# ScalarE's copy of the scores of two steps on, put in front of the odd head's sign with the 32nd value

## The chip, the cores and the metric

One Trainium2 chip, one of its cores. The metric is device time in microseconds (us) of one execution. TensorE (PE) multiplies matrices into PSUM and transposes, VectorE (DVE), ScalarE (ACT) and GpSimd (POOL) work on elements, SyncE (SP) issues transfers. Each engine takes its instructions strictly in the order in which they were written for it; semaphores make one engine wait for another.

## The reference

Attention of 8 batches x 8 heads over 576 positions, head size 64, in which each query keeps only its 32 largest scores; then a mixture of 8 experts, one expert a token. Cut to what matters:

```python
scores = scale * np.matmul(q, k.transpose(0, 1, 3, 2))
kth = np.partition(scores, -32, axis=-1)[..., -32:-31]      # the 32nd largest of each row
scores = np.where(scores >= kth, scores, -1e9)
attn = np.exp(scores - scores.max(-1, keepdims=True))
attn = attn / (attn.sum(-1, keepdims=True) + 1e-9)
x = np.matmul(attn, v)                                      # then as (4608, 512) rows
...
e_idx = np.argmax(x @ w_gate, axis=1)                       # one expert of 8 a row
h = np.maximum(x[mask] @ w1[e], 0.0)
out[mask] = gate_w[mask, None] * eom[mask, e, None] * (h @ w2[e])
```

## The kernel before

**Tiles and steps.** The queries are cut into 36 tiles of 128 rows, and the 8 heads of a tile into 4 pairs, an even and an odd head each. One pass of the main loop, a step i of 144, starts the work of pair i and finishes that of the pairs before it. When a group of tiles is through, its rows are sent to the experts, and slots of 128 rows of one expert are worked between the attention of later tiles. Steps 0 to 39 come before the first slots; in the code they are `calm` (`i < LONE`, and `LONE` is 40). The change touches these alone.

**What a pair passes through.** TensorE multiplies queries and keys into the PSUM tile `ps` (`scores`, L282); there is only one such tile. ScalarE copies it to SBUF as `s`, both heads in one instruction of 128 x 1152 (the function that `scores` returns, L290); four `s` tiles take turns. VectorE takes the 8 largest of each of 8 pieces of a row (`gmax`, L309, 16 instructions) and ranks these into the largest 24 (`rank`, L317 and L320). With the 24th value as a bias ScalarE marks the elements near or above it and counts them (`below`, the sign L344, one for each head), GpSimd adds the marks to the scores (L347, into `w`), VectorE takes the 8 largest of the result (`window`, L359) and picks the 32nd value by the count (`spot` L370, `pick` L376, `choose` L382). GpSimd scales the row's largest value to the offset of the exponent (`shift`, L333), ScalarE forms exponentials (`exps`, L354).

For the even head VectorE multiplies the exponentials with the mask and sums them (`weigh`, L397). In the calm steps the odd head goes another way, that of `lone`: `choose` writes its 32nd value negated (`less`, L385); `veil` has ScalarE take the sign of score minus that value (L404) and GpSimd add it to the scores (L407, into `w`); a step later `unveil` has ScalarE form the exponentials of the result with their sum (L413). TensorE transposes the exponentials (`flip`, L424, in three parts; ScalarE copies each out, L432) and multiplies them with the values (`attend`, L456; ScalarE copies the result out as `xT`, L458).

**One calm step i on ScalarE**, as the code writes it: the two signs L344 of pair i, the first part's copy L432, `unveil(i - 2)` (L413), `exps(i)` (L354), in every other step the copy of `xT`, the second part's copy L432, in some steps small copies for the gates (L479, L489); then what the change touches: `veil(i - 1)` (L404) and what the list `last` holds, the copy of the scores of pair i + 2 (L290) and the third part's copy (L432).

**On the other engines.** TensorE, in the same step, has the middle part's transpose, which needs `unveil(i - 2)`, directly in front of the products L282 of pair i + 2. VectorE ends its step with `pick`, `choose` and `weigh` of pair i - 1 and begins the next with `rank` of pair i + 1. GpSimd ends the step with the add L407 of pair i - 1, and begins the next with `shift`, in some steps a scaling of output rows (L498), and the pair of adds L347:

```order
L387 COPY near_78<-v32_1358 128x4
L407 TENSOR_TENSOR w_1602<-s_1243,marks2_81 128x576
L333 TENSOR_SCALAR v32_1575<-v32_1575 128x2
L498 TENSOR_TENSOR xu_1287<-xu_1287,r_1286 128x256
L347 TENSOR_TENSOR w_1622<-s_1451,marks0_79 128x576
```

These rows of GpSimd, from the end of one step into the next (a second L347 follows), stand so in both kernels: whatever lets L407 start later holds up what is behind it.

The list `last` is filled and emptied in these lines:

```python
            if calm and i + 2 < NSTEP:
                last.append(scores(i + 2))
...
            if 1 <= i <= NSTEP:
                veil(i - 1)
            for f in last:
                f()
```

Of the kernel before, what the change touches and what calls it, by code (L numbers as in the profile page):

```python
# [38 lines left out]
def tile_topk_attention_moe(  # L39
# [152 lines left out]
    def run(exact, stack):  # L192
# [30 lines left out]
        def run_slow(budget, kinds):  # L223

            for x in [x for x in slow if x[2] in kinds]:
                if spent[0] + x[3] > budget:
                    return
                slow.remove(x)
                spent[0] += x[3]
                x[4]()  # L230
# [10 lines left out]
        def fill(n=1):  # L241
            for _ in range(n):
                if urgent:
                    urgent.popleft()()
                elif small and small[0]() is not False:
                    small.popleft()
# [24 lines left out]
        def scores(i):  # L271
            t, hp = divmod(i, NHP)
            ps = ps_s.tile([P, 2, 2, 512], F32, name="ps")
            two = len(TT[t]) == 2
            for n in range(2):
                cols = slice(n * 288, (n + 1) * 288)

                for m, (b, _) in enumerate(TT[t]):
                    qs = slice(m * 64, (m + 1) * 64) if two else slice(0, P)
                    for a in range(2):  # L280
                        rows = slice(a * 64, (a + 1) * 64)
                        nc.tensor.matmul(ps[qs, a, n, :288], Q[t][rows, hp, qs], K[b][rows, hp, cols],  # L282
                                         start=True, stop=True)
            s = wk.tile([P, 2, S], F32, name="s", bufs=4)
            for a in range(2):
                SC[i, a] = s[:, a, :]

            def copies(heads=((0, 2),)):
                for a0, a1 in heads:
                    nc.scalar.activation(s[:, a0:a1].rearrange("p a (n c) -> p (a n) c", n=2),  # L290
                                         ps[:, a0:a1].rearrange("p a n c -> p (a n) c")[:, :, :288], AF.Copy)
            return copies
# [18 lines left out]
        def rank(i, r):  # L311
            if exact:
                return
            vs, cs = VV[i]
            cs = [c.rearrange("p (g k) -> p g k", k=8)[:, :, :REACH[r]] for c in cs]
            for a in range(2):
                nc.vector.max(out=vs[:, a, 8 * r:8 * r + 8], in_=cs[a])  # L317
            if r < 2:
                for a in range(2):
                    nc.vector.match_replace(out=cs[a], in_to_replace=vs[:, a, 8 * r:8 * r + 8],  # L320
                                            in_values=cs[a], imm_value=LOW)
# [9 lines left out]
        def shift(i):  # L331
            vs = VV[i][0]
            nc.gpsimd.tensor_scalar(vs[:, :, 32], vs[:, :, 0], -SCALE, None, op0=ALU.mult)  # L333

        def below(i):
            vs = VV[i][0]
            ep = wk.tile([P, 2, S], F32, name="ep", bufs=3)
            EP[i] = ep
            if not exact:
                n = wk.tile([P, 2], F32, name="n", bufs=3)  # L340
                SW[i] = ([], n)
                for a in range(2):
                    s, m = SC[i, a], marks[a]
                    nc.scalar.activation(m.bitcast(I8).rearrange("p (s b) -> p s b", b=2)[:, :, 1], s, AF.Sign,  # L344
                                         bias=vs[:, a, PIVOT - 1:PIVOT], scale=-(1.0 + 2.0 ** -20), accum_out=n[:, a:a + 1])
                    w = wk.tile([P, S], F32, name="w", bufs=3)
                    nc.gpsimd.tensor_tensor(w, s, m, op=ALU.add)  # L347
                    SW[i][0].append(w)
# [474 lines left out]
        NSTEP = NTT * NHP  # L823
# [115 lines left out]
        for i in range(NSTEP + 4):  # L939
            t, hp = divmod(i, NHP)  # L940
            step[0] = i
            if i + 1 < NSTEP and (i + 1, 0) not in SC:
                scores(i + 1)()


            calm = i < LONE and not exact
            for r in range(3):
                if i < NSTEP:
                    rank(i, r)
                    if r == 0:  # L950
                        shift(i)
                if not calm:
                    fill(1)
            spent[0] = 0.0
            run_slow(SUMS, ("x",))
            spent[0] = 0.0
            if i < NSTEP:
                below(i)
            early, late, last = [], [], []
            mid, beside = None, None  # L960
            if calm and 2 <= i:
                first_copy = flip(i - 2, 0)
                mid = ps_t.tile([P, 4, P], F32, name="pst")
                f = side_start()
                beside = f(mid) if f else None
                first_copy()
            if 2 <= i < NSTEP + 2:
                unveil(i - 2)
            if calm:
                exps(i)  # L970
            if 4 <= i < NSTEP + 4 and i % 2 == 0:
                early.append(attend(i - 4))
            elif 2 <= i < LONE:

                idle = ps_m.tile([P, 4, P], F32, name="pm")
                for c in range(12 if beside else 24):
                    nc.tensor.transpose(idle[:, c % 4, :], ident, ident)
            if mid is not None:
                early.append(flip(i - 2, 1, beside, mid))
            elif 2 <= i < NSTEP + 2:  # L980
                early.append(flip(i - 2, 0))
                early.append(flip(i - 2, 1, side_start()))
            if calm and i + 2 < NSTEP:
                last.append(scores(i + 2))
            if i >= NSTEP + 2:
                extra = side_start()
                if extra:
                    early.append(extra(ps_t.tile([P, 4, P], F32, name="pst")))

            room = not uses  # L990
            ahead_of_slot()
            heavy_start()
            ev = heavy_piece()
            if ev:
                late.append(ev)
            if 2 <= i < NSTEP + 2:
                (last if calm else late).append(flip(i - 2, 2))
            ev = turn_ahead() if room or not heavy else None
            if ev:
                (last if calm else late).append(ev)  # L1000
            for f in early:
                f()
            if i < NSTEP and not calm:
                exps(i)
            for f in late:
                f()
            if 1 <= i <= NSTEP:
                spot(i - 1)
                window(i - 1, 0)
                window(i - 1, 1)  # L1010
            if i + 1 < NSTEP:
                gmax(i + 1, 0)
            if i + 1 < NSTEP:
                gmax(i + 1, 1)
            if 1 <= i <= NSTEP:
                pick(i - 1)
            if not calm:
                fill(1)
            if 1 <= i <= NSTEP:
                choose(i - 1)  # L1020
                fill(5 if calm else 1)
                weigh(i - 1)
            ahead("x", fetch_x, 2, "id", 1)
            run_slow(DMAS - 0.6 if calm else DMAS, ("ids", "out"))
            if 1 <= i <= NSTEP:
                veil(i - 1)
            for f in last:
                f()
            side_use()
            fill(3)  # L1030
            if i < NSTEP:
                if hp == 0 and t + 2 < NTT:
                    load_q(t + 2)
                if i == 0:
                    small.extend(([] if exact else setup()) + [clear_ids])
                jj = t % 9
                b2 = t // 9 * 2
                for j0, b in ((0, b2 + 1), (5, b2 + 2)):
                    n = (jj - j0) * NHP + hp
                    if b < NB:  # L1040
                        if n == 1:
                            load_k(b)
                        if n == 6:
                            load_v(b)
            if i >= 3 and (i - 3) % NHP == NHP - 1:
                tt = (i - 3) // NHP
                if tt == GROUPS[gi][0]:
                    LGT[gi] = st.tile([P, max(map(len, GROUPS)), 16], F32, name="lg", bufs=2)
                tile_rows(tt, gi, LGT[gi], tt - GROUPS[gi][0])
                if tt == GROUPS[gi][-1]:  # L1050
                    gi += 1
# [263 lines left out]
```

## Time and profile before

| | |
|---|---|
| time, median of 3 runs | 1270.94 us (1270.91 to 1271.02) |
| the profiled execution's own time | 1270.56 us |
| its span, first to last instruction | 1268.8 us |
| TensorE busy | 1178.6 us, 93% |
| VectorE busy | 1178.5 us, 93% |
| ScalarE busy | 1021.7 us, 81% |
| GpSimd busy | 692.0 us, 55% |
| the sign L404 | 40 instructions, 19.5 to 282.7 us |

A row of the timeline has the start and the duration in us, the engine, the line, the operation, out<-in and a count, and in brackets the idle time in front of it with what ended that. Where a row stands for several instructions, the duration is that of all of them. A row of the waits has who waited for whom, the total in us, how often, and the longest. A row of windows has a stretch in us, the busy time of each engine with the number of instructions, the granted TensorE clock and the share of the transfers. Instructions of one engine overlap at their ends by about 0.1 us, so the start of one to the start of the next is what it occupies.

### The profile page before, as it was taken

What the parts mean: (1) busy time and instruction counts of PE and PEld (TensorE: products, weight loads), DVE (VectorE), ACT (ScalarE), POOL (GpSimd) and SP (SyncE); (2) the same over time, 40 slices, a digit from 0 to 9 for tenths busy, and PEclk for the clock granted to TensorE, in tenths of its full rate; (3) what the DMA queues carried; (4) which work ended last, traced back from release to release, by engine and by line L of the source; (5) the groups of instructions that cost most, each with busy time, mean ns of one, the idle gap of its engine ahead of it and who ended that gap; (6) DMA issues with size and microseconds to landing.
All of it is one profiled execution on the core that took longest, in us unless ns stands there. A gap on an engine that the chain in (4) does not pass through costs nothing.

```text
span 1268.8 us, 30920 instructions
## 1 busy us (share of the span) xinstructions
PE 1178.6 (93%) x9769; PEld 894.7 (71%) x9769; DVE 1178.5 (93%) x6045; ACT 1021.7 (81%) x1958; POOL 692.0 (55%) x1048
## 2 busy tenths in 40 slices
PE   6887778879999999999999999999999999899996
PEld 5665555557777777777777777777777777678885
DVE  7999999999999999999999999999999994689984
ACT  6999999987888778878888888878888884388883
POOL 6666676674467665664564475456556663232110
PEclk8999999988999999999999999999999999899998
DMA  5400210237446555656557556554444445899981
GB/s 138 78 18 18 72 56 18 56 118 245 167 165 204 174 203 179 215 192 222 183 197 228 189 184 204 182 202 167 167 167 167 167 165 213 317 376 396 391 310 60
DMA packets 109376, 227.39 MB, mean 179 GB/s; under 512 B 14855, under 2 KB 33543, under 8 KB 108177
## 3 DMA queue, kind: packets, MB, share of 16 engines
q1 hardware_dynamic: 99824, 205.67, 47.0%
q0 software_dynamic: 7552, 18.96, 4.2%
q8 instruction: 79, 1.29, 0.4%
q10 hardware_dynamic: 1824, 0.67, 0.3%
q14 instruction: 97, 0.79, 0.2%
HBM read 206.68 MB, written 20.69 MB: 179 GB/s over the span
## 4 chain that ended last, share of the span: by engine, by line
DVE 66%; PE 15%; issue 11%; ACT 5%; POOL 1%; DMA 1%; DVEq 0%; POOLq 0%; SPq 0%; ACTq 0%
DVE cand L309 20%; DVE v L359 12%; DVE ep L397 11%; DVE cand L320 7%; DVE v L317 6%; PE pm L786 4%; PE po L456 3%; DVE x L376 2%; PE ps L282 2%; DVE x L370 2%; DVE kth L382 2%; PE pst L424 1%; PE pm L801 1%; PE pm L1107 1%; ACT marks L344 1%
## 5 line engine op out<-in xcount | busy, mean ns | idle before, releaser
L347 POOL TENSOR_TENSOR w<-s,marks 128x576 f32<-128x576 f32 x288 | 363.3, 1283 | 202.6 <-ACT marks L344 183.1
L309 DVE MAX8 cand<-s 128x8 f32<-128x72 f32 x2304 | 321.9, 216 | 12.9 <-ACT s L290 12.8
L424 PE MATMUL pst<-ident,ep 128*128 128x128 f32 x1296 | 206.3, 283 | 46.0 <-ACT ep L413 32.5
L344 ACT ACTIVATE marks<-s,v 128x576 int8<-128x576 f32 x288 | 220.6, 770 | 23.8 <-DVE v L317 21.7
L432 ACT ACTIVATE pT<-pst 128x512 f32<-128x512 f32 (+1 forms) x432 | 197.7, 483 | 51.8 <-PE pst L424 50.4
L424 PEld LDWEIGHTS pst<-ident,ep 128*128 128x128 f32 x1296 | 145.5, 141 | 132.9 <-issue 48.7
L786 PE MATMUL pm<-xs,w1t 128*128 128x128 f32 x1792 | 212.3, 277 | 0.0
L786 PEld LDWEIGHTS pm<-xs,w1t 128*128 128x128 f32 x1792 | 206.7, 194 | 0.2 <-issue 0.2
L359 DVE MAX8 v<-w 128x8 f32<-128x576 f32 x288 | 203.3, 746 | 0.0
L397 DVE SCALAR_TENSOR_TENSOR ep<-s,kth,ep 128x576 f32<-128x576 f32 x248 | 194.8, 817 | 8.6 <-DVE kth L382 0.5
L290 ACT ACTIVATE s<-ps 128x1152 f32<-128x1152 f32 (+1 forms) x145 | 162.2, 1120 | 50.3 <-PE ps L282 49.9
L801 PE MATMUL pm<-w2t,ht 128*128 128x512 f32 x432 | 194.4, 593 | 0.0
L456 PE MATMUL po<-pT,v 128*64 128x128 f32 (+3 forms) x3200 | 186.4, 268 | 0.0
L282 PE MATMUL ps<-kst,qst 64*128 64x288 f32 (+1 forms) x1280 | 179.5, 428 | 5.2 <-ACT s L290 5.2
L354 ACT ACTIVATE ep<-s,v 128x576 f32<-128x576 f32 x248 | 181.0, 779 | 3.1 <-POOL v L333 3.1
L456 PEld LDWEIGHTS po<-pT,v 128*64 128x64 f32 (+1 forms) x3200 | 159.0, 137 | 33.7 <-issue 31.9
L812 POOL DMA_INDIRECT out_dram<-y,idt x40 | 45.6, 1140 | 160.5 <-ACT y L808 147.8
L801 PEld LDWEIGHTS pm<-w2t,ht 128*128 128x128 f32 x432 | 78.0, 191 | 77.5 <-issue 77.5
L317 DVE MAX8 v<-cand 128x8 f32<-128x24 f32 (+2 forms) x864 | 132.2, 194 | 0.0
L282 PEld LDWEIGHTS ps<-kst,qst 64*128 64x128 f32 (+1 forms) x1280 | 97.0, 176 | 44.2 <-issue 17.5
L320 DVE MATCH_REPLACE8 cand<-v,cand 128x24 f32<-128x24 f32 (+1 forms) x576 | 97.5, 178 | 0.0
L333 POOL TENSOR_SCALAR v<-v 128x2 f32<-128x2 f32 x144 | 32.8, 227 | 113.8 <-DVE v L317 112.7
(185 smaller groups left out, 1689.6 us busy)
## 6 DMA issues: line engine op xcount, KB each, us to landing
w1t<-in_w_dram SPq DMA_DIRECT2D x40, 2048.0 KB
w2t<-in_w_dram SPq DMA_DIRECT2D x40, 2048.0 KB
v<-in_va_dram SPq DMA_DIRECT2D x8, 1152.0 KB
x_rows<-xu SPq DMA_DIRECT2D x36, 256.0 KB
qst<-in_qa_dram SPq DMA_DIRECT2D x70, 128.0 KB
kst<-in_ka_dram SPq DMA_DIRECT2D x14, 576.0 KB
ids<-far SPq DMA_DIRECT2D x1, 678.0 KB
xg<-x_rows,idt POOLq DMA_INDIRECT x40, 6.4
```

The costliest lines, as they stand in the source:

```text
L282: nc.tensor.matmul(ps[qs, a, n, :288], Q[t][rows, hp, qs], K[b][rows, hp, cols], start=True, stop=True)
L309: nc.vector.max(out=c[:, 8 * g:8 * g + 8], in_=SC[i, a][:, g * GW:(g + 1) * GW])
L317: nc.vector.max(out=vs[:, a, 8 * r:8 * r + 8], in_=cs[a])
L344: nc.scalar.activation(m.bitcast(I8).rearrange("p (s b) -> p s b", b=2)[:, :, 1], s, AF.Sign, bias=vs[:, a, PIVOT - 1:PIVOT], scale=-(1.0 ...
L347: nc.gpsimd.tensor_tensor(w, s, m, op=ALU.add)
L359: nc.vector.max(out=VV[i][0][:, a, 24:32], in_=SW[i][0][a])
L397: nc.vector.scalar_tensor_tensor(e, SC.pop((i, a)), kth_col(i, a), e, op0=ALU.is_ge, op1=ALU.mult, accum_out=SM[t][:, 2 * hp + a:2 * hp + ...
L424: nc.tensor.transpose(ps[:, c - c0, :], pt[:, c * P:(c + 1) * P], ident)
L432: nc.scalar.activation(x, ps[:, :n, :], AF.Copy)
L456: nc.tensor.matmul(po[a * 64:(a + 1) * 64, k, qs], lhs, rhs, start=half and not k and not m, stop=(c == 3 and k == 1 and m == len(TT[t]) - 1))
L786: nc.tensor.matmul(ph[:, f - f0, :], w[:, c, f * P:(f + 1) * P], XS[s][:, c, :], start=(c == 0), stop=(c == NC - 1))
L801: nc.tensor.matmul(PY[s], HT[s][:, f, :], w[:, f, :], start=(f == 0), stop=(f == NF - 1))
```

## The change

In the calm steps the first entry of `last`, which is the copy of the scores of pair i + 2, is called ahead of `veil(i - 1)`. The other entries stay behind it.

```diff
             ahead("x", fetch_x, 2, "id", 1)
             run_slow(DMAS - 0.6 if calm else DMAS, ("ids", "out"))
+            if last and calm and i + 2 < NSTEP:
+                last.pop(0)()
             if 1 <= i <= NSTEP:
                 veil(i - 1)
             for f in last:
                 f()
```

On ScalarE, at the end of the same step and into the next (the numbers are those of the tiles; `s_1243` is pair i - 1, `s_1563` pair i + 2), the kernel before has

```order
L354 ACTIVATE ep_1513<-s_1344,v32_1465 128x576
L432 ACTIVATE pT1_1557<-pst_1527 128x128
L404 ACTIVATE marks2_81<-s_1243,less_1596 128x576
L290 ACTIVATE s_1563<-ps_1558 128x1152
L432 ACTIVATE pT4_1569<-pst_1564 128x512
L344 ACTIVATE marks0_79,n_1620<-s_1451,v32_1575 128x576
```

and the changed one

```order
L354 ACTIVATE ep_1513<-s_1344,v32_1465 128x576
L432 ACTIVATE pT1_1557<-pst_1527 128x128
L290 ACTIVATE s_1563<-ps_1558 128x1152
L404 ACTIVATE marks2_81<-s_1243,less_1596 128x576
L432 ACTIVATE pT4_1569<-pst_1564 128x512
L344 ACTIVATE marks0_79,n_1620<-s_1451,v32_1575 128x576
```

The copy, which waits for TensorE's products, now stands ahead of the sign, which waits for VectorE's `less`; the sign has moved one place back. The same exchange is made 39 times, in steps 1 to 39; step 0 has no sign. The order on the other engines is the same in both kernels.

## The prediction

> **What bounds the kernel now.** I read the chain that ended last first, then busy time by stage, then the waits of each engine in the stage that the change touches (steps 0 to 39, up to about 276 us), and last one step instruction by instruction. The chain by engine, a stretch of the stage by windows (PE, PEld, DVE, ACT, POOL, then PE clock and DMA), and the waits there (total us, times, longest):
>
> ```profile
> DVE 66%; PE 15%; issue 11%; ACT 5%; POOL 1%; DMA 1%; DVEq 0%; POOLq 0%; SPq 0%; ACTq 0%
> ...
> 30.00:144.00 114.00, 91.75 (x944) 68.07 (x943) 112.49 (x684) 109.39 (x236) 76.81 (x102) 1.00 0.22 47
> ...
> DVE cand L309 <- ACT s L290: 0.6, 1, 0.6
> ...
> ACT marks L344 <- DVE v L317: 8.2, 11, 3.8
> ACT marks L404 <- DVE less L385: 6.4, 8, 1.8
> ...
> ACT s L290 <- PE ps L282: 0.7, 3, 0.2
> ```
>
> VectorE is busy 112.49 of 114 us and, from 30 to 340 us, waits once, 0.6 us. ScalarE is nearly as full, 109.39 of 114. So VectorE sets the pace and ScalarE has little room. The sign waits now and then for VectorE's negated 32nd value; the copy behind it hardly ever waits for its products (0.7 us in all), because the sign fills the time in which TensorE makes them.
>
> One step on ScalarE, with the starts of the same instruction one and four steps on:
>
> ```profile
> 47.95 0.78 ACT L344 ACTIVATE marks<-s,v 128x576 int8<-128x576 f32 x1
> ...
> 49.94 0.77 ACT L413 ACTIVATE ep<-w,v 128x576 f32<-128x576 f32 x1
> ...
> 50.70 0.77 ACT L354 ACTIVATE ep<-s,v 128x576 f32<-128x576 f32 x1
> ...
> 51.63 0.28 ACT L432 ACTIVATE pT<-pst 128x128 f32<-128x128 f32 x1
> 52.06 0.78 ACT L404 ACTIVATE marks<-s,less 128x576 int8<-128x576 f32 x1
> 52.74 1.11 ACT L290 ACTIVATE s<-ps 128x1152 f32<-128x1152 f32 x1
> 53.75 0.59 ACT L432 ACTIVATE pT<-pst 128x512 f32<-128x512 f32 x1
> 54.23 0.77 ACT L344 ACTIVATE marks<-s,v 128x576 int8<-128x576 f32 x1
> ...
> 67.36 0.78 ACT L344 ACTIVATE marks<-s,v 128x576 int8<-128x576 f32 x1 [0.31 <-DVE v L317]
> ...
> 73.99 0.78 ACT L344 ACTIVATE marks<-s,v 128x576 int8<-128x576 f32 x1
> ```
>
> Four steps take 73.99 - 47.95 = 26.04 us, 6.51 a step. The other engines in that step, and the two VectorE rows that go with 67.36:
>
> ```profile
> 50.86 0.33 PE L424 MATMUL pst<-ident,ep 128*128 128x128 f32 x1 [1.19 <-ACT ep L413]
> 51.12 1.24 PE L282 MATMUL ps<-kst,qst 64*128 64x288 f32 x8
> ...
> 52.98 1.28 POOL L407 TENSOR_TENSOR w<-s,marks 128x576 f32<-128x576 f32 x1 [1.44 <-ACT marks L404]
> 54.23 0.22 POOL L333 TENSOR_SCALAR v<-v 128x2 f32<-128x2 f32 x1
> 55.18 2.52 POOL L347 TENSOR_TENSOR w<-s,marks 128x576 f32<-128x576 f32 x2 [0.73 <-ACT marks L344]
> ...
> 67.14 0.61 POOL L498 TENSOR_TENSOR xu<-xu,r 128x256 f32<-128x256 f32 x1
> ...
> 52.62 0.26 DVE L317 MAX8 v<-cand 128x8 f32<-128x24 f32 x2
> ...
> 53.99 0.30 DVE L370 TENSOR_TENSOR x<-left,n 128x16 f32<-128x16 f32 x1
> 54.22 1.41 DVE L359 MAX8 v<-w 128x8 f32<-128x576 f32 x2
> 55.55 2.23 DVE L309 MAX8 cand<-s 128x8 f32<-128x72 f32 x16
> 57.70 0.16 DVE L376 TENSOR_TENSOR x<-x,v 128x16 f32<-128x16 f32 x1
> ...
> 65.95 0.26 DVE L317 MAX8 v<-cand 128x8 f32<-128x24 f32 x2
> ```
>
> The reader is to see two things. First, TensorE's products (L282) stand behind a transpose that starts only 0.92 us after the exponential L413 of the same step, so their end is tied to ScalarE itself. Second, VectorE's small compare L370 took 0.30 us and ended, at 54.29, with GpSimd's add L407 (52.98 + 1.28 = 54.26). That is no accident of one step:
>
> ```profile
> L370 DVE TENSOR_TENSOR x<-left,n x39: 157/303/868, 15.4 to 270.7; 128x16 f32<-128x16 f32 x39
> ...
> 30.00:276.00 246.00, 10.05 (x36) 0.98 0.17 42
> ...
> 277.20 1.29 POOL L407 TENSOR_TENSOR w<-s,marks 128x576 f32<-128x576 f32 x1
> ...
> 277.30 1.23 DVE L370 TENSOR_TENSOR x<-left,n 128x16 f32<-128x16 f32 x1
> ```
>
> (L370 alone: shortest, median and longest in ns, then its busy time in a window.) L370 needs 0.157 us and on average takes 10.05/36 = 0.28; where the add began 0.10 us ahead of it, it took 1.23 and ended at 278.53, the add at 278.49. A two-input VectorE instruction that meets a running GpSimd add waits for its end. The next instruction starts 0.04 ahead of that end (54.22 against 54.26).
>
> **The change, part by part.** No instruction is added or removed; 39 times the copy L290 and the sign L404 change places on ScalarE, and nothing moves on the other four engines or on the queues of transfers.
>
> The copy, first. From L344 (time 0) the exponential starts at 49.94 - 47.95 = 1.99; the transpose 0.92 later, the products 0.26 after it, and they last 1.24. A copy that waits for them starts 0.05 after their end:
>
> ```profile
> 262.00 1.24 PE L282 MATMUL ps<-kst,qst 64*128 64x288 f32 x8
> ...
> 263.29 1.14 ACT L290 ACTIVATE s<-ps 128x1152 f32<-128x1152 f32 x1 [0.24 <-PE ps L282]
> ```
>
> So it starts at 1.99 + 0.92 + 0.26 + 1.24 + 0.05 = 4.46. That is only 0.28 earlier than the 52.74 seen, for ScalarE comes free near 51.9 and now stands still until 52.41 with the sign queued behind. The earlier copy buys nothing: today's ends at 53.85 and its reader L309 starts at 55.55, 1.70 later.
>
> The sign, second. The copy occupies 1.01 (52.74 to 53.75), the sign starts at 5.47 and occupies 0.68 (52.06 to 52.74), the next copy 0.48 (53.75 to 54.23). The next L344 can start at 6.63 at the earliest, 0.12 above today's 6.51. In today's order the sign starts at 4.11; now it is 1.36 later, and GpSimd's add with it: it starts 0.92 after the sign (52.06 to 52.98), at 6.39, and ends at 7.67.
>
> The compare, third. L370 comes 1.37 after the step's first L317 (52.62 to 53.99), L344 1.41 after it where it waits for it (65.95 to 67.36), so L370 tries 0.04 ahead of L344. At steps of 6.63 that is 6.59, behind the add's start at 6.39: it is blocked to 7.67 instead of for today's tenth of a microsecond. This delays the next step's ranking, hence the next L344, which delays that step's sign. From the release to the following L344 VectorE needs one period less what lies between L317 and L359, plus 1.41. In the step shown that stretch is 54.22 - 52.62 = 1.60 with a compare of 0.30, so 1.58 on average: 6.51 - 1.58 + 1.41 = 6.34. An L344 therefore comes 7.67 - 0.04 + 6.34 = 13.97 after the one two steps earlier: 6.98 a step. This fits itself: 6.98 is above ScalarE's 6.63, and a compare at 6.94 still meets the add (6.39 to 7.67) and waits 0.73. The cost is 0.47 a step, 39 x 0.47 = 18.3 us.
>
> Against that stands the routing work, which lengthens some steps on VectorE alone:
>
> ```profile
> 14.02 0.30 DVE L317 MAX8 v<-cand 128x8 f32<-128x24 f32 x2
> ...
> 275.93 0.27 DVE L317 MAX8 v<-cand 128x8 f32<-128x24 f32 x2
> ```
>
> Steps 1 to 39 last 261.91 us, 8.0 more than 39 x 6.51. While L370 is blocked, such work fills the wait: in the two-step sum it counts half. One step holds some 3.8 of it (the longest wait for L317 above), which can save no more than about one block, 0.7; of the other 4.2 half is saved, 2.1. The sum is 18.3 - 2.8 = 15.5 us.
>
> Costed at nothing: the later L333 (to 7.86, so 0.88 after the next L344; its reader L354 starts 2.75 after it); the later w for L413, 1.3 us in hand; L376, which comes 3.48 after L359, at about 4.1 after L344, where the pair L347 ends at 0.95 + 2.52 = 3.5, or at 4.0 in steps where the scaling L498 (0.61) stands between L333 and it. That last cover is thin, about 0.1; where it is gone L376 is blocked by the rest of the pair.
>
> The bounds of the one unknown, the copy's start: if the products were ready when ScalarE is free (3.95), the add ends at 7.16, the step is 6.73, and with half of the routing work saved the total is +6; if they always ran at the low clock below, each start is 1.05 later. I take 4.46, whose rows are of this very stage.
>
> On GpSimd's durations the Trainium skill (Perfetto Trace Analysis, GPSIMD Engine Instruction) says that reported spans are unreliable and start-to-start spacing is to be used. By that the add takes 1.25 (52.98 to 54.23), and the sum is 0.6 lower; by the row at 277.30 the span holds to 0.04.
>
> The delay should reach the end whole: VectorE has 66% of the chain and the later steps hang on it. Against the profiled execution's 1270.56 us (the median of the runs is 0.38 above) this gives 1286.
>
> **The rivals.**
>
> *Only ScalarE's own loop counts.* If the add and the compare settle so that they don't meet, a step is 6.63: at most 39 x 0.12 = 4.7, and the 8.0 of routing work lets ScalarE catch up. That gives 1271 to 1275. For it: ScalarE's lag has 1.7 us of cover at L309. Against it: at 6.63 the compare falls 0.20 behind the add's start. Chance 10%, two thirds of it within 0.2%, which is about what a measurement can tell from no change.
>
> *Faster.* The compare passes ahead of the add, and its waits go: (0.28 - 0.157) x 39 = 4.8 us, 1266. It decides at a compare ahead of 6.39, a step of at most 6.43, which needs the products 0.2 earlier than their rows. Chance 5%.
>
> *TensorE's clock falls.* Longer steps leave it idle for longer. Its clock did fall once after a thin stretch, and products then took 2.29:
>
> ```profile
> 226.00:229.00 3.00, 1.99 (x19) 1.75 (x17) 3.00 (x17) 2.49 (x7) 1.84 (x4) 1.00 0.02 5
> 229.00:232.00 3.00, 2.09 (x13) 1.25 (x13) 2.86 (x19) 1.78 (x6) 1.63 (x4) 1.00 0.00 0
> ...
> 235.00:238.00 3.00, 3.00 (x32) 3.00 (x32) 2.93 (x21) 2.53 (x6) 2.59 (x3) 0.52 0.68 186
> ...
> 290.24 2.29 PE L282 MATMUL ps<-kst,qst 64*128 64x288 f32 x8
> ```
>
> That puts the add 1.05 later, 0.53 a step: in half of the steps 10 us more, 1296, in all 1307. Chance 10%. The Trainium skill (TensorE: Matmul & The Clock Gate, HAM oscillation) has the clock fall only after idle gaps beyond about 3.4 us; by that it would not fall here and this rival had no chance. The rows differ: the two slices before the fall were idle for 1.01 and 0.91, no gap of 3.4.
>
> *The swap does nothing* needs ScalarE to take the two out of order; no row shows that, and it goes with the first rival.
>
> **How the numbers follow.** The forecast has 75%, the three rivals 10, 5 and 10. Slower by over 0.2% is the forecast, the clock's rival and a third of the first: 0.75 + 0.10 + 0.03 = 0.88; same is the rest of the first, 0.07; faster 0.05. The range runs from the low bound of the copy's start, +6, to the forecast with the clock down in a third of the steps: 1277 to 1293.
>
> **What would show it.** In the changed profile, in this stage: L290 waits for L282 in most steps, about 0.5 us; L404 no longer waits for L385; L370's median is near 0.9 us, and its ends lie 0.03 behind those of L407; the stage's steps are near 7.0 us; L309 waits no more than now. If L370 stays near 0.3 the third step of the sum is wrong; if L290 doesn't wait, the first. A granted clock well below 0.98 speaks for the third rival.

## The result and the profile after

The changed kernel takes 1286.78 us (median of 4 runs, 1285.30 to 1288.65) against 1270.93 (1270.37 to 1271.02): 15.9 us or 1.26% slower, ratio 1.0126, 95% interval 1.0109 to 1.0144. The forecast was 1286.0. The profiled execution took 1287.09, its span is 1285.3, 16.5 longer than the span before. "Stage" below means the time from the first L317 of the first row here to that of the second, as in the prediction; it went from 261.91 to 278.40, by the same 16.5. The delay arises there and is carried to the end whole. The stage's ends on VectorE, in the timeline of the changed kernel:

```profile
13.96 0.30 DVE L317 MAX8 v<-cand 128x8 f32<-128x24 f32 x2
...
292.36 0.27 DVE L317 MAX8 v<-cand 128x8 f32<-128x24 f32 x2
```

The chain by engine on the page of the profile, and a stretch by windows (PE, PEld, DVE, ACT, POOL, then PE clock and DMA):

```profile
DVE 68%; PE 15%; issue 10%; ACT 4%; POOL 1%; DMA 1%; DVEq 0%; POOLq 0%; SPq 0%; ACTq 0%
```

```profile
30.00:144.00 114.00, 85.39 (x834) 62.71 (x834) 112.69 (x630) 102.51 (x220) 73.39 (x100) 1.00 0.22 46
```

VectorE is as busy as it was, 112.69 of 114 us, yet it issues 630 instructions there instead of 684. It does not wait more; its instructions have become longer. ScalarE was busy 109.39 and is now busy 102.51. Its waits in the changed kernel from 14 to 290 us (total, times, longest):

```profile
ACT s L290 <- PE ps L282: 19.3, 35, 1.0
ACT marks L344 <- DVE v L317: 12.6, 20, 4.1
...
ACT marks L404 <- DVE less L385: 0.8, 1, 0.8
```

The copy now waits for its products in 35 steps, 0.55 each, and the sign no longer waits for `less`. These are ScalarE's waits. Where VectorE's time went is read from its groups of the stage (count, total us, mean ns, idle before). Before:

```profile
L397 DVE SCALAR_TENSOR_TENSOR ep<-s,kth,ep 128x576 f32<-128x576 f32 x39 | 31.2, 801 | 0.0
...
L370 DVE TENSOR_TENSOR x<-left,n 128x16 f32<-128x16 f32 x39 | 11.7, 300 | 0.0
L376 DVE TENSOR_TENSOR x<-x,v 128x16 f32<-128x16 f32 x39 | 7.0, 179 | 0.0
```

After:

```profile
L397 DVE SCALAR_TENSOR_TENSOR ep<-s,kth,ep 128x576 f32<-128x576 f32 x39 | 33.7, 864 | 0.0
...
L370 DVE TENSOR_TENSOR x<-left,n 128x16 f32<-128x16 f32 x39 | 21.8, 560 | 0.0
L376 DVE TENSOR_TENSOR x<-x,v 128x16 f32<-128x16 f32 x39 | 13.2, 340 | 0.0
```

The compare L370 costs 10.1 us more, the pick L376 6.2, the weighting L397 2.5, and two small routing instructions (L581, L627) 2.2 less: 16.6 in all, against 16.5 of the stage. All other large groups on VectorE are as before within 0.1 us. So the whole growth of VectorE's time lies in instructions that read two operands from SBUF. Whether that is the cause of the loss, or only what VectorE does while ScalarE is late, these sums can't say; the experiments are to decide it.

One step of the changed kernel, across the engines:

```profile
100.47 0.76 ACT L413 ACTIVATE ep<-w,v 128x576 f32<-128x576 f32 x1
...
101.63 1.24 PE L282 MATMUL ps<-kst,qst 64*128 64x288 f32 x8
...
102.98 1.13 ACT L290 ACTIVATE s<-ps 128x1152 f32<-128x1152 f32 x1 [0.83 <-PE ps L282]
...
104.01 0.77 ACT L404 ACTIVATE marks<-s,less 128x576 int8<-128x576 f32 x1
...
104.92 1.28 POOL L407 TENSOR_TENSOR w<-s,marks 128x576 f32<-128x576 f32 x1 [2.23 <-ACT marks L404]
...
105.20 1.04 DVE L370 TENSOR_TENSOR x<-left,n 128x16 f32<-128x16 f32 x1
```

The products end at 102.87, the copy follows 0.11 later, the sign 1.03 after that, GpSimd's add another 0.91, and 0.28 into the add comes the compare. It ends at 106.24, the add at 106.20. This is the prediction's picture. But 14 of the 39 compares took 0.16 us, and in ten of these steps the pick is caught instead:

```profile
169.73 0.16 DVE L370 TENSOR_TENSOR x<-left,n 128x16 f32<-128x16 f32 x1
...
170.33 1.28 POOL L407 TENSOR_TENSOR w<-s,marks 128x576 f32<-128x576 f32 x1 [3.57 <-ACT marks L404]
170.56 0.78 ACT L344 ACTIVATE marks<-s,v 128x576 int8<-128x576 f32 x1
...
171.75 2.52 POOL L347 TENSOR_TENSOR w<-s,marks 128x576 f32<-128x576 f32 x2
...
173.29 1.01 DVE L376 TENSOR_TENSOR x<-x,v 128x16 f32<-128x16 f32 x1
```

ScalarE is so late here that the compare passes ahead of the add. But L344 is then late as well: it comes 0.83 after the compare instead of 0.04. GpSimd's pair of adds L347 runs until 174.27, and the pick runs into it and ends at 174.30. Six steps in a row, from 31 to 67 us, went this way, and four later ones; in three the weighting was caught. In those six steps L344 never waits; the next one follows after 6.69 us each time, and after the last of them after 6.90.

```profile
36.60 0.78 ACT L344 ACTIVATE marks<-s,v 128x576 int8<-128x576 f32 x1
...
43.29 0.78 ACT L344 ACTIVATE marks<-s,v 128x576 int8<-128x576 f32 x1
```

There ScalarE's own loop sets the pace, and VectorE's wait at the pick costs nothing.

### The profile page after: what moved, and what is told of

It is laid out like the page before. It is cut to its first block, busy times and chain, and to the rows that moved or that the text cites. A ratio compares the mean times of both kernels' runs of the same rounds, so it can differ in the third digit from the quotient of the medians.

```text
span 1285.3 us, 30922 instructions
## 1 busy us (share of the span) xinstructions
PE 1180.2 (92%) x9769; PEld 893.9 (70%) x9769; DVE 1194.8 (93%) x6045; ACT 1022.7 (80%) x1958; POOL 691.1 (54%) x1048
## 4 chain that ended last, share of the span: by engine, by line
DVE 68%; PE 15%; issue 10%; ACT 4%; POOL 1%; DMA 1%; DVEq 0%; POOLq 0%; SPq 0%; ACTq 0%
DVE cand L309 21%; DVE v L359 12%; DVE ep L397 11%; DVE cand L320 7%; DVE v L317 6%; PE pm L786 5%; DVE x L376 3%; PE po L456 3%; DVE x L370 3%; PE ps L282 2%; DVE kth L382 2%; PE pst L424 1%; PE pm L801 1%; PE pm L1109 1%; ACT marks L344 1%
## 5 line engine op out<-in xcount | busy, mean ns | idle before, releaser
L347 POOL TENSOR_TENSOR w<-s,marks 128x576 f32<-128x576 f32 x288 | 363.0, 1282 | 187.0 <-ACT marks L344 169.1
L309 DVE MAX8 cand<-s 128x8 f32<-128x72 f32 x2304 | 321.9, 216 | 13.6 <-ACT s L290 13.6
L344 ACT ACTIVATE marks<-s,v 128x576 int8<-128x576 f32 x288 | 220.6, 770 | 26.5 <-DVE v L317 24.7
L397 DVE SCALAR_TENSOR_TENSOR ep<-s,kth,ep 128x576 f32<-128x576 f32 x248 | 197.3, 827 | 8.6 <-DVE kth L382 0.5
L317 DVE MAX8 v<-cand 128x8 f32<-128x24 f32 (+2 forms) x864 | 132.1, 194 | 0.0
L407 POOL TENSOR_TENSOR w<-s,marks 128x576 f32<-128x576 f32 x40 | 51.3, 1281 | 81.1 <-ACT marks L404 81.0
```

The source lines that it names most:

```text
L309: nc.vector.max(out=c[:, 8 * g:8 * g + 8], in_=SC[i, a][:, g * GW:(g + 1) * GW])
L397: nc.vector.scalar_tensor_tensor(e, SC.pop((i, a)), kth_col(i, a), e, op0=ALU.is_ge, op1=ALU.mult, accum_out=SM[t][:, 2 * hp + a:2 * hp + ...
```

## The experiments

The theory put to the test: GpSimd's adds end later because the sign starts later, and an instruction of VectorE with two operands in SBUF waits for them. The rival: ScalarE's 19.3 us of waiting for products is the loss, and the blocked instructions only fill time that VectorE would spend waiting anyway. "Regular step" is the mean of steps 9 to 20: 6.54 us in the kernel before, 7.07 in the changed one. Times are medians of at least 4 runs, beside runs of the kernel before on the same chip (medians 1270.06, 1270.44 and 1270.78).

**The waits taken away: products ahead of the middle transpose.** In the changed kernel (e3_early_after) and, as a control, in the kernel before (e4_early_before):

```diff
+            if calm and i + 2 < NSTEP:
+                last.append(scores(i + 2))
             if mid is not None:
                 early.append(flip(i - 2, 1, beside, mid))
...
-            if calm and i + 2 < NSTEP:
-                last.append(scores(i + 2))
```

> The change, and TensorE makes the products of pair i + 2 ahead of the middle part's transpose, so that they don't hang on the exponential L413. Theory (the price is VectorE's compare and pick meeting GpSimd's later adds): ScalarE's waits for products, 19.3 us in the changed kernel, go; the copy starts near 3.9 us after L344, the add runs from 5.8 to 7.1, the compare at 6.66 still meets it, a step is (7.1 - 0.04 + 6.34)/2 = 6.70: about 1276 us, and L370 still takes clearly more than 0.157 us. Rival (the 19.3 us of waiting on ScalarE are the loss of 16 us): all of it comes back, 1271 us.

> The kernel before, with the same earlier products and the sign still ahead of the copy. The copy hardly waited for products there (0.7 us in all), and the add starts when it did. Both theories: 1270 to 1272 us. It shows what the earlier products do by themselves.

The first took 1284.69 us (two runs at 1280 and 1281, two at 1288; ratio 1.0125, 1.0095 to 1.0156), the second 1283.84 (1.0104, 1.0087 to 1.0121). A wait of ScalarE and a group of VectorE in the first, whose profiled execution was the fastest of its four:

```profile
ACT marks L344 <- DVE v L317: 16.9, 27, 3.3
```

```profile
L370 DVE TENSOR_TENSOR x<-left,n 128x16 f32<-128x16 f32 x39 | 20.8, 533 | 0.0
```

The copy's wait for products is gone from the list, and the time is not back. The regular step is 6.75, where the theory had 6.70. The compare still takes 20.8 us in all, and L344 waits for VectorE 27 times, where it waited 20 times in the changed kernel. The totals of both forecasts were missed, for the edit has a price of its own. In the control the copies of the transposed weights wait for a transpose that now stands behind the products, and every fourth regular step is longer, up to 9.07 us:

```profile
ACT pT L432 <- PE pst L424: 19.3, 21, 1.8
```

So the waits went and the loss stayed, but since the edit by itself costs the control 13.8 us, the pair of runs doesn't decide between theory and rival.

**The block taken away: the compare's operands in PSUM.** Steps 0 to 39 keep the constant and the result of the compare in PSUM. An idle tile was freed for it (the filling transposes write to another). The edit was made in the kernel before (e11_psum_before) and in the changed one (e12_psum_after):

```diff
+        held = ps_m.tile([P, 4, P], F32, name="pm")
+        nc.vector.tensor_copy(held[:, 0, :8], left)
...
-            X8[i] = wk.tile([P, 2, 8], F32, name="x8", bufs=2)
-            nc.vector.tensor_tensor(X8[i], left[:, None, :].to_broadcast([P, 2, 8]),
+            near_by = step[0] < LONE
+            if near_by:
+                X8[i] = held[:, 1 + i % 2, :16].rearrange("p (a k) -> p a k", a=2)
+            else:
+                X8[i] = wk.tile([P, 2, 8], F32, name="x8", bufs=2)
+            nc.vector.tensor_tensor(X8[i], (held[:, 0, :8] if near_by else left)[:, None, :].to_broadcast([P, 2, 8]),
```

> The kernel before, with the constant of the compare L370 and the result of compare and pick kept in a PSUM tile in the calm steps, so that compare and pick read only one operand from SBUF (the pm tile is free there once TensorE's filling transposes write into po). The same instructions in the same order. Theory: a VectorE instruction is blocked by GpSimd's adds only when it reads two operands from SBUF; the 0.12 us of blocking a step go: 1265 to 1271 us, L370 all alike. Rival: 1271 us.

> The change, with compare and pick reading one operand from PSUM in the same way. ScalarE's order and its waits for products stay (about 20 us). Theory (the loss is VectorE blocked by the later adds): what is left is ScalarE's loop of 6.63 us a step, caught up in the steps with routing work: 1271 to 1277 us. Rival (the 20 us of waits for products are the loss): 1286 us.

The kernel before gains 5.4 us by it (1265.08; ratio 0.9958, 0.9941 to 0.9974), the changed one 9.9 (1276.88; 1.0054, 1.0037 to 1.0071). The groups of the first, in which the weighting is L403:

```profile
L403 DVE SCALAR_TENSOR_TENSOR ep<-s,kth,ep 128x576 f32<-128x576 f32 x39 | 31.2, 801 | 0.0
...
L376 DVE TENSOR_TENSOR pm<-pm,n 128x16 f32<-128x16 f32 x39 | 6.4, 164 | 0.0
```

The groups and a wait of the second (compare L376, pick L382):

```profile
L403 DVE SCALAR_TENSOR_TENSOR ep<-s,kth,ep 128x576 f32<-128x576 f32 x39 | 41.5, 1065 | 0.0
...
L376 DVE TENSOR_TENSOR pm<-pm,n 128x16 f32<-128x16 f32 x39 | 6.4, 164 | 0.0
L382 DVE TENSOR_TENSOR pm<-pm,v 128x16 f32<-128x16 f32 x39 | 6.4, 163 | 0.0
```

```profile
ACT s L290 <- PE ps L282: 21.5, 36, 1.6
```

This refutes the rival for the larger part of the loss. ScalarE keeps the changed order and waits 21.5 us for products, and 9.9 of the 15.9 us are back; 1276.88 is the upper end of the theory's range.

What is left is ScalarE's own loop, as the theory had it, and in this loop the waits for products do count. The first L344 of each step, in three steps in a row, without an idle time in front:

```profile
82.49 0.78 ACT L344 ACTIVATE marks<-s,v 128x576 int8<-128x576 f32 x1
...
89.18 0.78 ACT L344 ACTIVATE marks<-s,v 128x576 int8<-128x576 f32 x1
...
96.08 0.78 ACT L344 ACTIVATE marks<-s,v 128x576 int8<-128x576 f32 x1
```

It comes every 6.69 us, and after 6.90 in every fourth step; the forecast for this loop was 6.63. From 30 to 250 us it does not wait for VectorE at all here. In the changed kernel it does, in the same stretch:

```profile
ACT marks L344 <- DVE v L317: 6.2, 15, 0.9
```

So the exchange lengthens two loops, and in the changed kernel the one through VectorE's blocked instructions is the longer. With compare and pick freed the kernel runs at ScalarE's pace. That is why the exchange still costs 11.8 us between these two kernels: the regular step is 6.37 us in the first and 6.75, at ScalarE's pace, in the second. The stages differ by 11.5 (254.86 and 266.40).

The block itself is not gone in the second. Compare and pick run free in both, but the next instruction with two operands in SBUF, the weighting, has grown by 10.3 us:

```profile
97.84 2.51 POOL L347 TENSOR_TENSOR w<-s,marks 128x576 f32<-128x576 f32 x2
...
98.98 0.16 DVE L382 TENSOR_TENSOR pm<-pm,v 128x16 f32<-128x16 f32 x1
...
99.45 1.52 DVE L403 SCALAR_TENSOR_TENSOR ep<-s,kth,ep 128x576 f32<-128x576 f32 x1
...
100.30 0.72 POOL L393 COPY near<-v 128x4 f32<-128x4 f32 x1
```

The pick runs in 0.16 us in the midst of the pair of adds; the weighting has to wait for the pair's end at 100.35 and ends 0.62 later. The block passes on to the next such instruction. But since L344 does not wait for VectorE in this stretch, this block sets no pace and is not the cause of the 11.8 us.

On this the Trainium skill (SBUF — State Buffer, Who interferes with whom) says that a VectorE instruction with two SBUF inputs and a GpSimd instruction that reads SBUF exclude each other, while one with at most one SBUF input, outside certain fast modes, doesn't contend. The runs agree: the compare took 560 ns on average in the changed kernel and 164 ns once one operand was in PSUM.

**The sign later still.** In the changed kernel the sign goes behind the third part's copy as well, about half a microsecond (e5_sign_last):

```diff
             if last and calm and i + 2 < NSTEP:
                 last.pop(0)()
+                if last:
+                    last.pop(0)()
```

> The change taken one place further: the third part's copy L432 also stands ahead of the sign. ScalarE has the same instructions and the same loop through the products; only the sign, and with it the add, comes 0.48 us later (add 6.87 to 8.15 us after L344). Theory: a step is (8.15 - 0.04 + 6.34)/2 = 7.22 us, 0.24 more than forecast for the change: about 1295 us. Rival: the waits for products are the same, so the time stays at that of the change, 1287 us.

It took 1290.80 us (1286.57 to 1294.30; ratio 1.016, 1.0131 to 1.0189). The regular step is 7.28, where the theory had 7.22, with ScalarE's wait for products unchanged (20.2 us). The median is 4.0 above the changed kernel's, half of what the theory gave, and the two ranges overlap. Its groups:

```profile
L376 DVE TENSOR_TENSOR x<-x,v 128x16 f32<-128x16 f32 x39 | 20.1, 516 | 0.0
L370 DVE TENSOR_TENSOR x<-left,n 128x16 f32<-128x16 f32 x39 | 18.2, 466 | 0.0
```

More compares pass ahead of the add (the one at 105.85 took 0.16, the add came at 105.98), and the pick pays. The longer regular step is that of one profiled execution; the times alone don't separate this kernel from the changed one.

**The adds in four pieces**, so that a block would last a quarter, in the changed kernel (e8_split_after) and, as a control, in the kernel before (e9_split_before):

```diff
-                    nc.gpsimd.tensor_tensor(w, s, m, op=ALU.add)
+                    for c in range(4 if i < LONE else 1):
+                        k = slice(c * 144, (c + 1) * 144) if i < LONE else slice(0, S)
+                        nc.gpsimd.tensor_tensor(w[:, k], s[:, k], m[:, k], op=ALU.add)
...
```

> The change, with each of GpSimd's adds L347 and L407 of the calm steps cut into four pieces of 144 columns (the same elements, four times the instructions). A VectorE instruction that meets an add now waits for the end of a piece, some 0.35 us at most instead of 1.28. Theory: the blocks all but go and ScalarE's loop of 6.63 us is left: 1271 to 1277 us, with the waits for products on ScalarE still there. Rival: those waits are the loss, so 1286 us stay, or more, as GpSimd has more to do.

> The kernel before, with the same adds cut into four. Theory: of the compare's 0.12 us of blocking a step, most goes (39 x 0.1 = 4 us), and ScalarE, 6.28 us in the shortest steps, gives the new pace: 1267 to 1271 us. Rival: nothing on ScalarE changes, 1271 us.

Both forecasts failed: 1288.78 us (1.0138, 1.0120 to 1.0155) and 1286.05 (1.0122, 1.0105 to 1.0139). The stage of the first, 278.50, is that of the changed kernel. GpSimd in the control:

```profile
101.71 1.71 POOL L412 TENSOR_TENSOR w<-s,marks 128x144 f32<-128x144 f32 x4 [0.89 <-ACT marks L406]
...
104.14 3.37 POOL L349 TENSOR_TENSOR w<-s,marks 128x144 f32<-128x144 f32 x8
```

Four pieces take 1.71 us where the whole took 1.28, and eight take 3.37 where two wholes took 2.52. The edit lengthened the adds by a third instead of only dividing them. That makes the control worth more than it was meant to be: ScalarE's order is that of the kernel before, its copy hardly waits for products (0.2 us in all), and the kernel is 15 us slower by more and longer adds alone. The pick and the compare show it, and a wait on ScalarE, from 14 to 290 us (the sign is L406 here):

```profile
L378 DVE TENSOR_TENSOR x<-x,v 128x16 f32<-128x16 f32 x39 | 16.4, 419 | 0.0
L372 DVE TENSOR_TENSOR x<-left,n 128x16 f32<-128x16 f32 x39 | 16.0, 410 | 0.0
```

```profile
ACT marks L406 <- DVE less L387: 16.2, 24, 2.1
```

Pick and compare take 13.7 us more than the 7.0 and 11.7 of the kernel before, where the stage grew by 15.6. And here VectorE does hold up ScalarE: the sign waits 16.2 us for `less`, where it waited 6.4 in the kernel before. So longer adds make the kernel slower through VectorE, without a wait for products. Whether a shorter block by itself would help is left open, since the split didn't make one without longer adds.

**The compare elsewhere: behind L309, next to the pick.** In the changed kernel (e6_spot_after) and in the kernel before (e7_spot_before):

```diff
-                spot(i - 1)
+                if not calm:
+                    spot(i - 1)
...
+                if calm:
+                    spot(i - 1)
                 pick(i - 1)
```

> The change, with the compare L370 moved in the calm steps from ahead of the two L359 to behind the 16 L309, next to the pick L376. There it doesn't meet the single add L407; it can meet the pair L347, which ends late because it follows the add. Theory: L370's block by L407 goes, one by the pair takes part of its place; a step of 6.64 us without the scaling L498 on GpSimd and 6.95 with it, 6.8 on average: 1276 to 1281 us. Rival (waits for products are the loss): 1286 us.

> The kernel before, with the compare moved in the same way. The 0.12 us of blocking a step by L407 go, but at the new place, 0.3 us ahead of where L376 stands, the pair L347 still has 0.1 to 0.3 us to run. Theory: 1268 to 1272 us. Rival: 1271 us.

1284.10 us (1.0103, 1.0087 to 1.0120) and 1272.83 (1.0016, 1.0006 to 1.0026). The first gains 2.7 on the changed kernel, less than forecast; the second is 2.1 slower than the kernel before, 0.8 beyond the theory's range. The group of the first, and one step in its timeline:

```profile
L370 DVE TENSOR_TENSOR x<-left,n 128x16 f32<-128x16 f32 x39 | 20.7, 532 | 0.0
```

```profile
100.01 2.51 POOL L347 TENSOR_TENSOR w<-s,marks 128x576 f32<-128x576 f32 x2
...
101.78 0.77 DVE L370 TENSOR_TENSOR x<-left,n 128x16 f32<-128x16 f32 x1
```

The compare no longer meets the single add. But the pair comes late because the single add ahead of it is late; it ends at 102.52, the compare at 102.55. In its new place it is blocked as long as in the old one (20.7 us in all against 21.8). Moving the instruction did not avoid the block.

**Compare, pick and sum as one instruction for each head**, in the kernel before (e10_fused_before) and in the changed one (e13_fused_after), and with the constant in PSUM in steps 0 to 39 in the kernel before (e14_fused_psum_before):

```diff
-            nc.vector.tensor_tensor(X8[i], left[:, None, :].to_broadcast([P, 2, 8]),
-                                    SW[i][1][:, :, None].to_broadcast([P, 2, 8]), op=ALU.is_equal)
...
-            nc.vector.tensor_tensor(X8[i], X8[i], VV[i][0][:, :, 24:32], op=ALU.mult)
+            for a in range(2):
+                nc.vector.scalar_tensor_tensor(X8[i][:, a, :], left, SW[i][1][:, a:a + 1], VV[i][0][:, a, 24:32],
+                                               op0=ALU.is_equal, op1=ALU.mult,
+                                               accum_out=KTH[:, 2 * i + a:2 * i + a + 1])
...
-            nc.vector.tensor_reduce(KTH[:, 2 * i:2 * i + 2], X8.pop(i), axis=AX.X, op=ALU.add)
+            X8.pop(i)
```

> The kernel before, with compare L370, pick L376 and sum L382 made one instruction a head (scalar, compare, multiply, with a sum), at the pick's place, in all 144 steps. VectorE loses three instructions of 0.08, 0.19 and 0.20 us from start to start, and the compare's blocking, and gains two of about 0.2 us, an estimate. Theory: up to 0.2 us a step where VectorE sets the pace: in the calm steps about 8 us, and less in the later ones, where TensorE is full: 1255 to 1268 us. Rival: ScalarE's loop is as full as VectorE, so nothing comes of it, 1271 us.

> The change on top of the fused compare, pick and sum (which alone gave 1262 us). No compare stands at the add's place, but the fused pair stands behind the pair L347, which follows the late add; and ScalarE's loop of 6.63 us is above the 6.32 us that a regular step takes with the fusion. Theory: 6.65 to 6.7 a step, 39 x 0.35 less some 3 us: 1273 us. Rival (the change costs its waits whatever VectorE does): 1262 + 16 = 1278 us.

> The fused version of the kernel before, with the constant in PSUM in the calm steps, so that the fused instructions read one operand from SBUF and can't be blocked by the pair L347 (their mean was 0.23 us, shortest near 0.2). Theory: 0 to 2 us less than with the fusion alone, 1260 to 1263 us. Rival: reading PSUM costs more than the blocks, 1264 us.

1262.42 us (0.9932, 0.9916 to 0.9949), 1278.99 (1.0070, 1.0053 to 1.0087) and 1262.12 (0.9935, 0.9919 to 0.9952). The first and the third beat both kernels; between those two there is no difference that the runs can tell. The second missed the theory's 1273 and came out at the number that the rival had. The fused group of the first and that of the second, in this order:

```profile
L375 DVE SCALAR_TENSOR_TENSOR x<-left,n,v 128x8 f32<-128x8 f32 x78 | 15.3, 232 | 0.0
```

```profile
L375 DVE SCALAR_TENSOR_TENSOR x<-left,n,v 128x8 f32<-128x8 f32 x78 | 32.0, 445 | 0.0
```

The fused instructions take 16.7 us longer in the changed order, and the two medians differ by 16.6 (with the kernel before 0.3 apart beside them). It is tempting to take the one for the cause of the other. ScalarE's waits say otherwise; this is what L344 waits for VectorE in the second from 30 to 250 us:

```profile
ACT marks L344 <- DVE v L317: 0.4, 2, 0.2
```

It comes every 6.69 to 6.72 us in most steps and after 6.90 in every fourth, as with compare and pick in PSUM. ScalarE's loop, with its waits for products, sets the pace, and the blocked instructions fill time in which VectorE is ahead. So in this kernel the rival's account is the right one: the fusion makes VectorE faster, and in the changed order that can't be used. That its number came out as well is luck, for its 16 us are those of a kernel in which the other loop sets the pace. The theory had the right loop and too small a size for it, 6.65 to 6.7 us a step, where the regular step is 6.79.

## Why the prediction was right

The time, the sign and the mechanism came out: the copy waits for products, the sign and GpSimd's add come later, VectorE is held by the add, and the loop through both is longer than ScalarE's own. That the sum came as near as 1 us is partly luck.

- *The copy's start* (4.46 after L344, 2.47 after the exponential L413): 2.51 after L413 in the step shown. Right, with the waits of 0.55 in 35 steps.
- *The sign and the add* (1.01 behind the copy, 0.92 behind the sign): 1.03 and 0.91. Right.
- *ScalarE's own loop* (6.63): 6.69 where it sets the pace, as in the changed kernel from 37 to 63 us, and 6.90 in every fourth step. Slightly too short.
- *The compare* was forecast to be blocked in every step, with a median near 0.9 us. In 25 of 39 steps it was blocked, with a median over all of 0.56. L344 was taken to follow the compare by 0.04 in every step; in a third of the steps ScalarE itself was late, and the compare was already through.
- *The pick costed at nothing*, "cover thin, about 0.1": it had no cover in ten steps and took 6.2 us more. The prediction named the price (the rest of the pair) and left it out of the sum. What it cost the kernel is less than that: in six of the ten steps ScalarE's loop set the pace. The weighting's 2.5 us, three blocked instances, were not foreseen.
- *Why the sum still held*: the regular step is 7.07 against 6.98 forecast, an increase of 0.53 on 6.54 instead of 0.47. That would be 39 x 0.53 = 20.7 instead of 18.3; the stage grew by 16.5, so the other steps, those up to 67 us at ScalarE's pace among them, gave back 4.2 instead of 2.8. The two errors, 2.4 up and 1.4 down, have opposite signs; that is the luck.
- *The rivals*: ScalarE's loop alone was to end at 1275 at most. The kernel in which it does set the pace, with compare and pick in PSUM, took 1276.88, and the changed kernel lies 9.9 above that. The clock fell no further than before: it was 1.00 from 30 to 144 us in both kernels, and from 144 to 276 us 0.97 in the changed one and 0.96 in the one before. The row of 2.29 us that the prediction shows for this rival is not from the fall at 235 us but from a later stretch, 289 to 292 us, in which the clock was 0.50. Faster did not occur, though its condition did in part: 14 compares passed ahead of the add, but in ten of these steps the pick was caught instead.

What is not settled: what ends the stretch up to 67 us in which ScalarE's loop sets the pace, and why runs of the changed kernel spread over 3.35 us where those before spread over 0.65. Two loops of nearly the same length would give such a spread, but no run separates them.

## What to carry to other kernels

Where VectorE's short instructions read two operands from SBUF and GpSimd streams beside them, look at their mean duration against their shortest one: a mean of 300 ns over 157 is a queue, though no view of waits lists it. What then counts is when GpSimd's instruction ends, hence what it waits for.

But time that an engine shows as busy is not yet time that it costs. In two of the experiments the block passed on to another instruction of VectorE and grew there by 10 and by 17 us, while ScalarE set the pace. Which of the two it is shows on the other engine: look whether its first instruction of a step waits. A change of order can lengthen two loops at once, and when the longer one is freed, the other is what is left. And a cover of 0.1 us is none when the step itself is changed by several tenths.

## What the hardware showed

- The block is one of single instructions. In the kernel before, the pick got in between two adds that stood back to back:

```profile
1053.56 2.53 POOL L347 TENSOR_TENSOR w<-s,marks 128x576 f32<-128x576 f32 x2 [1.93 <-ACT marks L344]
...
1054.08 0.80 DVE L376 TENSOR_TENSOR x<-x,v 128x16 f32<-128x16 f32 x1
...
1055.21 1.49 DVE L397 SCALAR_TENSOR_TENSOR ep<-s,kth,ep 128x576 f32<-128x576 f32 x1
```

  The pick ended at 1054.88, where the first add of the pair would end (1053.56 + 1.28 = 1054.84), not at the pair's end of 1056.09. The weighting, which came next, met the second add and ended at 1056.70, 0.61 behind it.
- It works in the other direction too: GpSimd's copy of 128x4 takes 0.18 us where it runs free (at 102.51 in the changed kernel) and took 0.72 behind the weighting in the changed kernel with compare and pick in PSUM (the timeline shown there), ending at 101.02 where the weighting ended at 100.97.
- In the kernel before with split adds, GpSimd's add L349 of 128x144 has a mean of 461 ns, and four in a row take 1.71 us, so each starts 0.42 us after the one before it, against 1.28 us for 128x576. A quarter of the columns costs a third of the time. The Trainium skill (GPSIMD Engine Reference, Performance versus the Vector engine) gives 4497 ns for an add of 2048 columns of float32; an estimate in proportion to that would be 1265 ns for 576 columns, which agrees, and 316 for 144, which doesn't.
